# Where a block of the convolution's kernel opens within an attention step, and a ring of four PSUM banks once that kernel is done

## The chip, the cores and the metric

The kernel runs on one core of a Trainium2 chip. Its time is the device time in microseconds of one execution, and a lower time is better. TensorE is called PE below, VectorE DVE, ScalarE ACT, GpSimd POOL and SyncE SP. SP issues all of this kernel's DMA transfers. PSUM, which takes the results of matmuls, has eight banks of 128 x 512 float32, and each tile that this text names fills one bank.

## The reference, cut to what matters

Two independent operators work on sequences of length 2048 and width 448, and their outputs stand side by side.

```python
def _A_ref(u, log_A_real, A_imag, C_real, C_imag, log_dt, D_skip):
    dt = jnp.exp(log_dt)
    A = -jnp.exp(log_A_real) + 1j * A_imag
    C = (C_real + 1j * C_imag) * dt[:, None]
    P = jnp.exp((A * dt[:, None])[:, :, None] * pos[None, None, :])   # D x N x L
    K = 2.0 * jnp.einsum("dn,dnl->dl", C, P).real
    ...
    y = jnp.fft.irfft(Uf * Kf[None, :, :], L2)[:, :, :L]              # y = u convolved with K
    return y + u * D_skip[None, None, :]

def _B_ref(x, wqkv, wo):                                              # 16 heads of 28
    scores = jnp.einsum("bhqd,bhkd->bhqk", q, k) * scale
    o = jnp.einsum("bhqk,bhkd->bhqd", _softmax(scores), v)
    return o.reshape(B, S, D) @ wo
```

A makes a convolution kernel K from powers of complex numbers, and applies it in the frequency domain. B is multi-head attention.

## The kernel before

A first stage projects queries, keys and values, makes seeds for K, and leaves them in DRAM. Then comes one long loop, in which both operators are interleaved by hand: all engines keep the order in which the program issues their instructions.

**The loop.** It has 256 steps. A step handles one of 16 units (four heads times 512 queries) and one of 16 tiles of 128 keys. Within a step the tuple `ORDER` says what is issued:

```python
ORDER = ('m0', 's0', 'm1', 's1', 'v', 'f', 'pv', 'f', 'v', 'm2', 's2', 'm3', 's3', 'v')
```

- `s0` to `s3` (`s_mm`): one score matmul each into a `pss` bank, and ACT's exp of it into `p`.
- `m0` to `m3` (`max_mm`): four matmuls for the row maxima of a unit 19 steps ahead. `m0` (weights or keys named `kdif`) is read by ACT's Relu into `rl`; `m1` by DVE's combined add-and-max, which also reads `rl`; `m2` and `m3` by DVE's reductions into `mx`. This goes on while the step is below 237.
- `pv`: the product of the previous step's `p` with the values, into `po`.
- `f`: a free slot, which takes one task if one is due. In the order of the queue: urgent ends of a unit (row maxima `max_end`, with DVE's `mh`; `fin`, with sums, scaling and projections), matmuls of the convolution's kernel (`m_due`), stages of the transform of u (`u_due`, matmuls named `ua`), and the spectrum and final jobs of the convolution (`f_slot`).
- `v`: one group of DVE operations of the convolution's kernel, if one is queued.

**Blocks of the convolution's kernel.** There are 56 blocks, one every three or four steps (3.5 on average). `k_begin` opens a block at the head of a step, if the one before is through with its powers. Opening means `k_start`: three ACT copies, to `g`, to `zg` (a PSUM bank of its own, the pool `ps_g`) and to `e`. It queues nine groups for DVE (`g_powers`, one at each `v`; the lowest one needs the copies to `g` and `zg`) and nine products for POOL (`e_power`, three at the head of each of three steps, from the copy to `e`). Five steps later its matmuls (`e,g`, then `w,ko`) are due in free slots. `k_next`, at the end of a step, loads the next-but-one block's data (`sdb`) once the powers are issued.

**The ring of banks.** `w_tile` gives the next bank, in turn, to every `max_mm` and to every task in a slot. It has three banks, `pm0` to `pm2`, from the pool `ps_m`, which lives from the first stage to the end. PE waits where the bank's reader is not done. The eight banks of the loop are: three of `ps_m`, three of `ps_s` (`pss`), one of `ps_o` (`po`), one of `ps_g` (`zg`).

**Spectrum jobs.** Sixteen jobs run from about step 196 to 240, each of four tasks in slots. `forth(0)` and `last` each have 16 matmuls (`yk,mw`) into a ring bank, which DVE reads with two products `pr`. `last` then joins them: two operations `p` on DVE and two on POOL. After a gap, `back(0)` and `back(1)` (matmuls `p,mw`) are evacuated by ACT. Eight final jobs (`finish`, matmuls `zi,wb`, DVE's `ot`) follow as their spectrum is done. The block pool `g_p` is closed at the head of the first step at which nothing of the blocks is left, which is step 200.

The head and the end of a step's body before, as far as the change moves them:

```python
        k_begin(s)                       # L981, ahead of everything in the step
        ...
        for _ in range(3):               # L1003, three POOL products
            if powers["e"]:
                powers["e"].popleft()()
        ...
        k_next()                         # after the step's last operation
```

Of the kernel before, what the change touches and what calls it, by code (L numbers as in the profile page):

```python
# [7 lines left out]
F32 = mybir.dt.float32  # L8
# [5 lines left out]
PSUM = bass.MemoryType.PSUM  # L14
# [9 lines left out]
CQ = 512  # L24
# [5 lines left out]
NU = G * NQ  # L30
NS = NU * NK
LEAD = 3
ORDER = ('m0', 's0', 'm1', 's1', 'v', 'f', 'pv', 'f', 'v', 'm2', 's2', 'm3', 's3', 'v')
PB = 8
F1 = 2
FX, PD, GAP = 1, 2, 2
# [52 lines left out]
def body(ctx, tc, a, out):  # L89
# [5 lines left out]
    def pool(stack, name, bufs=1, space=None, side=None):  # L95
        kw = {} if space is None else {"space": space}
        if side:
            kw["side"] = side
        return stack.enter_context(tc.tile_pool(name=name, bufs=bufs, reuse_waits="tile", **kw))
# [18 lines left out]
    w1 = const.tile([128, 2, 128], F32, name="w1")  # L118

    att, k0_st = ExitStack(), ExitStack()  # L120
    ps_m = pool(att, "ps_m", 1, PSUM)
    n_ring = [0]

    def w_tile():

        n_ring[0] += 1
        return ps_m.tile([128, CQ], F32, name=f"pm{n_ring[0] % 3}")

    q_p = pool(att, "q_p", side="right")
    v_p = pool(att, "v_p", side="right")  # L130
# [18 lines left out]
    def load_v(g, c):  # L149
        v_g[g, c] = t = v_p.tile([128, NK // NQ, HG, 32], F32, name="v", bufs=5)  # L150
        nc.sync.dma_start(t.rearrange("p t h e -> p t (h e)"), v_d[c][:, g])
# [3 lines left out]
    def load_kd(g, j):  # L155
        kd_g[g, j] = t = kd_p[0].tile([128, CQ], F32R, name=f"kdif{j}")
        for r in range(4):
            nc.sync.dma_start(t[32 * r:32 * r + 32].bitcast(F32), kd_d[g][r % 2, 32 * j:32 * j + 32, :])
# [47 lines left out]
    with ExitStack() as st:  # L206
# [3 lines left out]
        x_p = pool(xst, "x_p")  # L210
        y_p = pool(wst, "y_p", side="right")
        w_p = pool(wst, "w_p", side="right")
        ps_t = pool(st, "ps_t", 2, PSUM)
        ps_n = pool(st, "ps_n", 2, PSUM)
        ps_x = pool(st, "ps_x", 1, PSUM)
# [327 lines left out]
    kq_st = ExitStack()  # L543
# [2 lines left out]
    g_p = pool(g_st, "g_p")  # L546
    ps_s = pool(att, "ps_s", 3, PSUM)
    ps_o = pool(att, "ps_o", 1, PSUM)
    ps_g = pool(att, "ps_g", 1, PSUM)
    k_pools = [k0_p, kq_p]  # L550

    late = [False]
# [50 lines left out]
    def load_sd(b):  # L603
        sds[b] = g_p.tile([128, SDF], F32, name="sdb", bufs=3)
        nc.sync.dma_start(sds[b], sd_d[b // BO][b % BO])

    def k_start(b):
        sd = sds[b]
        e = g_p.tile([128, 2, 16, N2], F32, name="e", bufs=2)
        g = g_p.tile([128, 2, 16, N1], F32, name="g", bufs=2)  # L610
        zg = ps_g.tile([128, CQ], F32, name="zg")
        egs[b] = e, g
        zgs[b] = zg
        nc.scalar.activation(g[:, :, :, :4], sd[:, F_G:F_Z].rearrange("p (c h e) -> p c h e", c=2, e=4), AF.Copy)
        nc.scalar.activation(zg[:, :Z_G], sd[:, SDF - Z_G:], AF.Copy)
        nc.scalar.activation(e[:, :, :, :8], sd[:, :F_G].rearrange("p (c h e) -> p c h e", c=2, e=8), AF.Copy)

    def e_power(b, i, q):

        t, m = egs[b][0], 8 << i  # L620
        zz = sds[b][:, F_Z:].rearrange("p (k f h) -> p k f h", k=6, f=3)
        if q == 0:
            zr = zz[:, i, 0, :][:, None, :, None].to_broadcast([128, 2, 16, m])
            nc.gpsimd.tensor_tensor(t[:, :, :, m:2 * m], t[:, :, :, :m], zr, ALU.mult)
        elif q == 1:
            uts[0] = g_p.tile([128, 2, 16, 32], F32, name="eu")[:, :, :, :m]
            zi = zz[:, i, 1:3, :][:, :, :, None].to_broadcast([128, 2, 16, m])
            nc.gpsimd.tensor_tensor(uts[0], t[:, ::-1, :, :m], zi, ALU.mult)
        else:
            nc.gpsimd.tensor_tensor(t[:, :, :, m:2 * m], t[:, :, :, m:2 * m], uts[0], ALU.add)  # L630

    def g_powers(b):

        t, zg = egs[b][1], zgs[b]
        zz = zg[:, :Z_G].rearrange("p (k f h) -> p k f h", k=3, f=3)
        tt = nc.vector.tensor_tensor

        def first(i, m):
            tt(t[:, :, :, m:2 * m], t[:, :, :, :m], zz[:, i, 0, :][:, None, :, None].to_broadcast([128, 2, 16, m]), ALU.mult)

        def second(i, m, c):
            n = c.stop - c.start
            u = zg[:, CQ // 2:CQ // 2 + n * 16 * m].rearrange("p (c h m) -> p c h m", c=n, m=m)
            zi = zz[:, i, 1 + c.start:1 + c.stop, :][:, :, :, None].to_broadcast([128, n, 16, m])
            tt(u, t[:, ::-1, :, :m][:, c], zi, ALU.mult)
            return lambda: tt(t[:, c, :, m:2 * m], t[:, c, :, m:2 * m], u, ALU.add)
        both, u = slice(0, 2), {}

        def lowest():
            first(0, 4)  # L650
            second(0, 4, both)()
        ops = [lowest, lambda: first(1, 8), lambda: u.update(a=second(1, 8, both)), lambda: u["a"](), lambda: first(2, 16)]
        for c in (slice(0, 1), slice(1, 2)):
            ops += [lambda c=c: u.update(a=second(2, 16, c)), lambda: u["a"]()]
        return ops
# [58 lines left out]
    def load_og(u):  # L714
        og_u[u] = og = kq_p.tile([128, G - 1, CQ], F32, name="og")
        nc.sync.dma_start(og, on_d[u % NQ][:G - 1].rearrange("g p q -> p g q"))
# [138 lines left out]
    powers = {"g": collections.deque(), "e": collections.deque()}  # L855
# [30 lines left out]
    f0_st, f1_st = ExitStack(), ExitStack()  # L886
# [62 lines left out]
    def k_begin(s_):  # L949
        if not (k_due and K0 + k_due[0] * KP <= s_ and done["mm"] >= k_due[0] - 2 and not powers["e"] and not powers["g"]):  # L950
            return
        b = k_due.popleft()
        k_start(b)
        powers["g"] += g_powers(b)
        powers["e"] += [lambda i=i, q=q: e_power(b, i, q) for i in range(3) for q in range(3)]
        p0, p1, p2 = k_mm(b)

        def m1():
            p1()
            done["mm"] = b  # L960
        m_due.extend((s_ + KD, t_) for t_ in (p0, m1, p2))
        last[0] = b
# [3 lines left out]
    def k_next():  # L966

        if last[0] is not None and not powers["e"] and not powers["g"]:
            if last[0] + 2 < NB:
                load_sd(last[0] + 2)  # L970
            last[0] = None

    def vec():
        if powers["g"]:
            powers["g"].popleft()()

    prev = None
    for s in range(NS):
        u, kt = divmod(s, NK)
        sm = s + NK + LEAD  # L980
        k_begin(s)  # L981
        if s == 12 * NK:
            k0_st.close()
            f_p["s", 0] = f_p["s", 1] = pool(f0_st, "f0_p", side="right")
            f_ready["s", 0], f_ready["s", 1] = s, NS
        if s >= 12 * NK and f_ready["s", 1] == NS and not (k_due or m_due or powers["g"] or powers["e"]):
            g_st.close()
            f_ready["s", 1] = s + F1
        if kt == 12 and u // NQ == G - 1:
            load_og(u)  # L990
        late[0] = s + NK + LEAD > NS
        if u % NQ == NQ - 1 and u < NU - 1 and kt % 4 == 2:
            load_v(u // NQ + 1, kt // 4)
        if sm < NS and sm // NK % NQ == NQ - 1 and sm % NK % 4 == 0 and sm % NK and sm // (NQ * NK) + 1 < G:
            load_kd(sm // (NQ * NK) + 1, sm % NK // 4 - 1)
        if sm < NS and sm % (NQ * NK) == 0 and sm:
            load_kd(sm // (NQ * NK), HG - 1)
        if kt % 4 == 1 and u % NQ == 1 and u // NQ + 1 < G:
            load_k(u // NQ + 1, kt // 4, k_pools[(u // NQ + 1) % 2])
        if kt == 2:  # L1000
            if u + 2 < NU:
                load_q(u + 2)
        for _ in range(3):  # L1003
            if powers["e"]:
                powers["e"].popleft()()
        ps = []
        for op in ORDER:
            if op[0] == "s":
                ps.append(s_mm(u, kt, int(op[1])))
            elif op[0] == "f":  # L1010
                slot(s)
            elif op[0] == "v":
                vec()
            elif op == "pv":
                if prev:
                    pv_step(*prev)
                    if prev[1] == NK - 1:
                        fin(prev[0], s)
            elif sm < NS:
                max_mm(sm // NK, sm % NK, int(op[1]))  # L1020
        for _ in range(FX if late[0] else 0):
            slot(s)
        if sm < NS and sm % NK == NK - 1:
            def end(un=sm // NK):
                max_end(un, w_tile())
                max_put(un)
            max_join(sm // NK)
            soon_slot(UG[0], end)
        k_next()
        prev = (u, kt, ps)  # L1030
    pv_step(*prev)
    fin(prev[0], NS)
    s = NS
# [1 line left out]
        slot(s)  # L1035
        s += 0.5
    assert not k_due and not powers["g"] and not powers["e"]
    for st in (f1_st, kq_st, f0_st, att):
        st.close()


# [55 lines left out]
```

## Time and profile before

| | us |
|---|---|
| median of three runs | 1427.25 (1426.0 to 1428.26) |
| profiled execution | 1427.0 |
| its span in the trace | 1425.2 |
| mean granted clock of PE | 0.961 of full |

In the trace, an instruction's row gives its start and length in us, the engine, and output and input tiles by name; in brackets stands how long the engine had idled and which instruction's end released it. A row "x4" merges neighbours of one kind. In a table of waits a row reads: who waited for whom, total us, times, longest. Matmul ends are modelled, so a busy PE is not a PE at its peak. Since helpers record every operation, all have line 73, and tiles tell them apart.

### The profile page before, as it was taken

The numbers are of one execution on the slowest core, as the hardware profiler recorded it, in microseconds if no ns is written. First come the engines' busy times: TensorE is split into PE (matmuls) and PEld (weight loads), VectorE is DVE, ScalarE is ACT, GpSimd is POOL, SyncE is SP. The second block draws the span as 40 slices with busy tenths as digits, with TensorE's granted clock in tenths as the row PEclk, the third lists the DMA queues.
The fourth block names the chain that finished last, engine by engine and source line by source line (L and its number), as shares of the span: only waits on it lengthen the run. The fifth ranks groups of instructions, "written<-read, shape, count | busy, mean of one in ns | idle before, by whom it ended". The sixth has DMA issues, their size and how long they took to land.

```text
span 1425.2 us, 33209 instructions
## 1 busy us (share of the span) xinstructions
PE 1273.5 (89%) x12625; PEld 707.7 (50%) x12625; DVE 978.6 (69%) x2138; ACT 974.4 (68%) x2069; POOL 830.8 (58%) x705
## 2 busy tenths in 40 slices
PE   6978856899999999999999999999988898898998
PEld 4756633445555555555555555555544444433433
DVE  5688766877778777777777878877786646645411
ACT  5867642688788888888787877878775545544553
POOL 3657650587778787778878878887861101102211
PEclk9998887899999999999999999999999999998999
DMA  6666679447663654586441316333244334435476
GB/s 190 236 235 216 225 267 249 112 98 180 150 149 85 152 151 122 157 200 165 140 91 40 92 36 150 89 79 84 55 136 134 112 106 144 154 110 164 134 199 175
DMA packets 200729, 205.37 MB, mean 144 GB/s; under 512 B 96632, under 2 KB 159160, under 8 KB 198520
## 3 DMA queue, kind: packets, MB, share of 16 engines
q1 hardware_dynamic: 200568, 203.23, 51.4%
q8 instruction: 100, 1.64, 0.5%
q14 instruction: 61, 0.50, 0.1%
HBM read 120.73 MB, written 82.18 MB: 142 GB/s over the span
## 4 chain that ended last, share of the span: by engine, by line
PE 58%; DVE 23%; ACT 7%; POOL 6%; issue 3%; DMA 3%; SPq 0%; ACTq 0%; DVEq 0%; POOLq 0%
PE pm L73 34%; PE po L73 13%; PE pss L73 11%; DVE mx L73 5%; DVE g L73 4%; DVE rl L73 3%; DVE p L73 3%; POOL qhat L73 3%; ACT p L73 2%; DVE pr L73 2%; ACT rl L73 2%; DVE tri L73 1%; DVE px L73 1%; DVE zg L73 1%; POOL x_e L73 1%
## 5 line engine op out<-in xcount | busy, mean ns | idle before, releaser
L73 ACT ACTIVATE p<-pss 128x512 f32<-128x512 f32 x1024 | 563.0, 607 | 162.4 <-PE pss L73 153.4
L73 DVE TENSOR_REDUCE mx<-pm 128x1 f32<-128x512 f32 x500 | 321.3, 683 | 141.5 <-PE pm L73 140.6
L73 PE MATMUL pss<-qhat,khat 128*128 128x512 f32 x1024 | 405.2, 402 | 3.2 <-ACT p L73 3.2
L73 PE MATMUL pm<-khat,qhat 128*128 128x512 f32 x749 | 335.3, 451 | 62.0 <-DVE mx L73 60.2
L73 POOL TENSOR_TENSOR e<-e,sdb 128x256 f32<-128x256 f32 x168 | 201.6, 1200 | 185.2 <-ACT e L73 129.6
L73 PE MATMUL po<-p,v 128*32 128x512 f32 x2048 | 278.8, 612 | 0.0
L73 PEld LDWEIGHTS pm<-khat,qhat 128*128 128x128 f32 x749 | 142.4, 190 | 247.3 <-DVE mx L73 114.9
L73 POOL TENSOR_TENSOR e<-e,eu 128x256 f32<-128x256 f32 x168 | 248.3, 1478 | 13.2
L73 DVE CUSTOM_DVE_ANT_0 rl<-pm,rl 128x512 f32<-128x512 f32 x249 | 171.5, 689 | 107.2 <-ACT rl L73 86.9
L73 PEld LDWEIGHTS pss<-qhat,khat 128*128 128x128 f32 x1024 | 192.0, 190 | 46.1 <-ACT p L73 12.8
L73 POOL TENSOR_TENSOR eu<-e,sdb 128x256 f32<-128x256 f32 x168 | 201.9, 1202 | 0.0
L73 POOL TENSOR_TENSOR p<-pr,pr 64x448 f32<-64x448 f32 x32 | 40.6, 1269 | 237.5 <-DVE pr L73 236.3
L73 ACT ACTIVATE rl<-pm 128x512 f32<-128x512 f32 x249 | 150.2, 603 | 32.3 <-PE pm L73 31.6
L73 DVE TENSOR_TENSOR g<-g,zg 128x128 f32<-128x128 f32 x392 | 162.7, 415 | 5.0
L73 PE MATMUL pm<-kdif,qhat 128*128 128x512 f32 x249 | 103.7, 417 | 14.9 <-DVE ot L73 4.0
L73 PEld LDWEIGHTS pm<-e,g 128*32 128x32 f32 x3584 | 64.0, 110 | 52.2 <-issue 34.2
L73 DVE TENSOR_TENSOR zg<-g,zg 128x128 f32<-128x128 f32 x224 | 87.3, 390 | 3.5
L73 ACT ACTIVATE y<-pm 128x448 f32<-128x448 f32 x48 | 26.3, 549 | 80.4 <-PE pm L73 54.1
L73 PEld LDWEIGHTS po<-p,v 128*32 128x32 f32 x2048 | 57.5, 111 | 43.8 <-issue 39.1
L73 PE MATMUL pm<-e,g 128*32 128x64 f32 x3584 | 72.8, 220 | 0.0
L73 PEld LDWEIGHTS pm<-kdif,qhat 128*128 128x128 f32 x249 | 47.3, 190 | 43.5 <-PE pss L73 9.7
L73 PE MATMUL pm<-xh,wh 112*128 112x512 f32 x128 | 54.5, 430 | 13.5 <-DVE tl L73 6.3
(137 smaller groups left out, 1545.8 us busy)
## 6 DMA issues: line engine op xcount, KB each, us to landing
sdb<-sd SPq DMA_DIRECT2D x56, 336.0 KB
qhat<-q SPq DMA_DIRECT2D x64, 256.0 KB
khat<-k SPq DMA_DIRECT2D x64, 256.0 KB
sd<-sg SPq DMA_DIRECT2D x8, 1456.0 KB
mw<-in_mw SPq DMA_DIRECT2D x16, 512.0 KB
sd<-qhat SPq DMA_DIRECT2D x8, 896.0 KB
yk<-yk SPq DMA_DIRECT2D x56, 128.0 KB
yu_d<-ub SPq DMA_DIRECT2D x64, 112.0 KB
```

The source lines that it names most:

```text
L73: i = f(*args, **kw)
```

## The change

The opening of a block moves into `ORDER` as an operation `k`, right behind `pv`. There `k_next`, `k_begin` and the three POOL products of the step are issued, so that they come between the step's two free slots. The ring's pool is no longer one for the whole kernel: the first stage has its own (`ps_w`), and the loop has `ps_m`, opened together with `ps_g`. At step 200, where `g_p` is closed, `ps_g` and `ps_m` are closed too, and a pool `ps_f` of four banks takes their place; from there `w_tile` gives one of its four in turn.

```diff
-ORDER = ('m0', 's0', 'm1', 's1', 'v', 'f', 'pv', 'f', 'v', 'm2', 's2', 'm3', 's3', 'v')
+ORDER = ('m0', 's0', 'm1', 's1', 'v', 'f', 'pv', 'k', 'f', 'v', 'm2', 's2', 'm3', 's3', 'v')
...
-    ps_m = pool(att, "ps_m", 1, PSUM)
-    n_ring = [0]
+    ps_w, n_ring = [None, 3], [0]
 
     def w_tile():
 
         n_ring[0] += 1
-        return ps_m.tile([128, CQ], F32, name=f"pm{n_ring[0] % 3}")
+        return ps_w[0].tile([128, CQ], F32, name=f"pm{n_ring[0] % ps_w[1]}")
...
         w_p = pool(wst, "w_p", side="right")
+        ps_w[0] = pool(st, "ps_w", 1, PSUM)
         ps_t = pool(st, "ps_t", 2, PSUM)
...
     ps_o = pool(att, "ps_o", 1, PSUM)
-    ps_g = pool(att, "ps_g", 1, PSUM)
+    ps_st = ExitStack()
+    ps_g = pool(ps_st, "ps_g", 1, PSUM)
+    ps_w[0] = pool(ps_st, "ps_m", 1, PSUM)
...
-        k_begin(s)
         if s == 12 * NK:
...
         if s >= 12 * NK and f_ready["s", 1] == NS and not (k_due or m_due or powers["g"] or powers["e"]):
             g_st.close()
+            ps_st.close()
+            ps_w[:] = pool(ps_st, "ps_f", 4, PSUM), 1
             f_ready["s", 1] = s + F1
...
-        for _ in range(3):
-            if powers["e"]:
-                powers["e"].popleft()()
         ps = []
         for op in ORDER:
...
             elif op[0] == "v":
                 vec()
+            elif op == "k":
+                k_next()
+                k_begin(s)
+                for _ in range(3):
+                    if powers["e"]:
+                        powers["e"].popleft()()
             elif op == "pv":
...
-    for st in (f1_st, kq_st, f0_st, att):
+    for st in (ps_st, f1_st, kq_st, f0_st, att):
         st.close()
```

`k_next()` at the end of the step in the kernel before stays where it is; behind a `k` that has already loaded, it finds nothing to do.

## The prediction

> **What bounds the kernel now.** I read the page's engine shares first, then busy time by stage, then the table of waits for the stages that the change touches, then the order of time inside single steps.
>
> ```profile
> span 1425.2 us, 33209 instructions
> ...
> PE 1273.5 (89%) x12625; PEld 707.7 (50%) x12625; DVE 978.6 (69%) x2138; ACT 974.4 (68%) x2069; POOL 830.8 (58%) x705
> ```
>
> TensorE (PE) is busy for 89% of the span, but that is a mean over unlike stages. The rows below are stretches of the attention loop: from us, to us, length, then busy time of PE, PEld, DVE, ACT and POOL, and the granted clock. The first two lie where blocks of the convolution's kernel are made (steps 0 to about 199), the third where the spectrum work runs (about 200 to 236).
>
> ```profile
> 480.00:690.00 210.00, 204.76 (x2380) 109.94 (x2373) 156.56 (x372) 174.76 (x409) 162.38 (x129) 1.00 0.59 159
> ...
> 870.00:1059.00 189.00, 176.08 (x2082) 98.18 (x2082) 150.03 (x357) 148.47 (x327) 157.81 (x123) 1.00 0.37 90
> ```
> ```profile
> 1079.00:1318.00 239.00, 205.12 (x1800) 99.01 (x1799) 136.79 (x237) 116.53 (x221) 33.25 (x26) 0.91 0.42 136
> ```
>
> Up to 690 us PE fills 204.8 of 210 us: both free slots of a step hold matmuls, and a late other engine rarely shows. From 690 to 1059 us the slots are half empty, and PE idles for 12.9 of 189 us while DVE, ACT and POOL each sit near 80%: here their order within the step decides. From 1079 us PE idles for 34 of 239 us, and its granted clock falls to 0.91. What ends PE's idle time there:
>
> ```profile
> PE pm L73 <- DVE mx L73: 24.0, 10, 2.5
> ...
> PE pm L73 <- DVE ot L73: 4.0, 1, 4.0
> PE pm L73 <- DVE pr L73: 3.2, 13, 0.3
> ...
> PE pm L73 <- DVE mh L73: 2.4, 1, 2.4
> ```
>
> Those 33.6 us are all PE waiting for DVE to release a `pm` bank. From 690 to 1059 us the same wait is shorter and more frequent, and DVE in turn waits for ACT's `rl`:
>
> ```profile
> DVE rl L73 <- ACT rl L73: 28.5, 46, 1.3
> ...
> PE pm L73 <- DVE mx L73: 24.4, 30, 1.2
> ```
>
> **Part 1: a block opens in the middle of a step.** PE's instruction order is unchanged, and so are the 56 opening steps (0, 4, 7, 11, ...: four and three steps apart in turn). What moves: `k_start`'s three ACT copies go from ahead of `rl` to behind the step's second exp and first free slot; the nine POOL products follow; the nine DVE groups start one `v` later, so the last one falls on the first `v` of the fourth step. `load_sd` is issued on SP about half a step later, behind that step's loads and first slot, for a block that opens at least three steps on; `sdb` has three buffers, so nobody waits for it. POOL's own order is kept and it starts later by under 2 us. Its products are used five steps after the opening, while they take under three, so that slack of about two steps (8 us) hides it; without it PE would pay the 2 us per block.
>
> One opening step four steps after the last, before the change:
>
> ```profile
> 881.57 0.31 ACT L73 ACTIVATE g<-sdb 128x128 f32<-128x128 f32 x1
> 881.77 0.30 ACT L73 ACTIVATE zg<-sdb 128x144 f32<-128x144 f32 x1
> ...
> 882.29 0.60 ACT L73 ACTIVATE rl<-pm 128x512 f32<-128x512 f32 x1
> ...
> 882.76 2.07 ACT L73 ACTIVATE p<-pss 128x512 f32<-128x512 f32 x4
> ...
> 882.91 0.69 DVE L73 CUSTOM_DVE_ANT_0 rl<-pm,rl 128x512 f32<-128x512 f32 x1 [1.32 <-PE po L73]
> ...
> 883.53 0.28 DVE L73 TENSOR_TENSOR g<-g,zg 128x128 f32<-128x128 f32 x1
> ...
> 884.18 0.74 DVE L73 TENSOR_TENSOR g<-g,zg 128x128 f32<-128x128 f32 x2
> ...
> 884.84 1.28 DVE L73 TENSOR_REDUCE mx<-pm 128x1 f32<-128x512 f32 x2
> ...
> 885.58 0.50 PE L73 MATMUL pm<-khat,qhat 128*128 128x512 f32 x1 [1.11 <-DVE mx L73]
> ```
>
> The copies hold ACT for 0.72 us (881.57 to 882.29), so DVE idles 1.32 us ahead of `rl`; the first powers and then `mx` come late, and PE stands 1.11 us for the bank that the first `mx` frees. Now with the change. `rl` takes the copies' place at 881.57; exps follow 0.47 us later (882.29 to 882.76) and 0.52 us apart (2.07/4): 882.04, 882.56; with an empty slot the copies start at 883.07, and `zg` (0.20 later, 0.30 long) ends at 883.57. DVE is through with `rl` by then, waits, and begins the lowest power at about 883.62 instead of 883.53. But in between it now has one group less: from 883.53 to the second power's start (884.18 + 0.28 + 0.04 = 884.50) are 0.97 us, after which `mx` starts: 884.59 less the small overlap, against 884.84. Gain about 0.27 us.
>
> Three steps after the last opening, `zg`'s copy had also to wait for the previous block's last addition on DVE:
>
> ```profile
> 893.38 0.41 DVE L73 TENSOR_TENSOR g<-g,zg 128x256 f32<-128x256 f32 x1
> 893.43 0.31 ACT L73 ACTIVATE g<-sdb 128x128 f32<-128x128 f32 x1
> ...
> 893.82 0.29 ACT L73 ACTIVATE zg<-sdb 128x144 f32<-128x144 f32 x1
> ...
> 896.89 1.28 DVE L73 TENSOR_REDUCE mx<-pm 128x1 f32<-128x512 f32 x2
> ```
>
> With the change: `rl` at 893.43, DVE's `rl` from 894.05, 0.61 later that addition (0.41, to 895.07); copies from 893.43 + 0.47 + 2 x 0.52 = 894.94, `zg` done by 895.43; lowest power 895.48, `mx` 896.45 against 896.89. Gain 0.44 us. From 690 us there are 26 openings, 13 of each kind: 13 x 0.27 + 13 x 0.44 = 9.2 us.
>
> Before 690 us the first slot mostly holds work that ACT evacuates, and that now stands ahead of the copies:
>
> ```profile
> 307.99 0.58 ACT L73 ACTIVATE ub<-pm 128x448 f32<-128x448 f32 x1
> ...
> 309.11 1.28 DVE L73 TENSOR_REDUCE mx<-pm 128x1 f32<-128x512 f32 x2
> ...
> 309.85 0.50 PE L73 MATMUL pm<-khat,qhat 128*128 128x512 f32 x1 [0.37 <-DVE mx L73]
> ```
>
> The evacuation pushes the copies back by its 0.5 us pace; the same count puts `mx` at 309.32, 0.21 us late, after a four-step gap, and level after a three-step gap. Of these 30 openings some have an empty slot and gain; I take 1 us lost, between 6 us lost (30 x 0.21) and 6 us gained.
>
> **Part 2: four PSUM banks for `w_tile`.** From step 200 (powers, products and their matmuls all done) `zg`'s bank joins the ring. The other pool moves only re-lay banks at the loop's start, on tiles long read: nothing, at most 1 us either way. In a ring of three, tile n waits for the reader of n-3; in a ring of four for n-4's, which the ring of three had already demanded one tile sooner. So no single wait gets longer. A stall at full clock, three steps ahead of the switch, serves as the measure:
>
> ```profile
> 1064.02 2.66 DVE L73 TENSOR_TENSOR p<-pr,pr 64x448 f32<-64x448 f32 x2
> ...
> 1066.61 1.27 DVE L73 TENSOR_REDUCE mx<-pm 128x1 f32<-128x512 f32 x2
> 1067.34 0.50 PE L73 MATMUL pm<-khat,qhat 128*128 128x512 f32 x1 [2.50 <-DVE mx L73]
> ...
> 1068.88 0.94 PE L73 MATMUL pm<-p,mw 128*32 128x224 f32 x16
> ```
>
> DVE joins the spectrum (2.66 us) ahead of `mx`, and PE's second `khat` matmul of the next step waits. With a fourth bank that matmul, its score matmul and, where the next slot is empty, `po` run during the joins; then the slot's `p,mw` needs that same `mx`. PE resumes at 1067.34 with `p,mw` instead of reaching it at 1068.88: 1.5 us gained, and the idle stretch shrinks from 2.5 to about 1.5 us. Of the ten `mx` stalls, four are of this kind (first slot of the next step empty). In the other six that slot needs the bank ahead of `po`: gain 0.7 us each (the `khat` and score matmuls with their weight loads), leaving 1.7 us idle where it was 2.15 (three) and 2.0 where it was 2.5 (three). The `mh` and `ot` stalls give 0.5 us each by the same move, and half of the `pr` waits 1.6 us. Sum: 4 x 1.5 + 6 x 0.7 + 2 x 0.5 + 1.6 = 12.8 us.
>
> The larger half may be the clock. These rows are consecutive stretches of 3.4 us, PE's busy time first, clock third from the end:
>
> ```profile
> 1082.90:1086.30 3.40, 1.46 (x6) 0.58 (x4) 3.35 (x4) 2.17 (x4) 2.53 (x2) 1.00 0.52 198
> 1086.30:1089.70 3.40, 2.58 (x10) 0.91 (x14) 2.06 (x5) 0.60 (x1) 0.00 (x0) 0.51 0.00 0
> 1103.40:1106.80 3.40, 1.75 (x22) 1.11 (x26) 2.89 (x5) 1.37 (x4) 0.51 (x1) 1.00 0.22 81
> 1106.80:1110.20 3.40, 3.40 (x32) 2.05 (x24) 1.39 (x3) 2.18 (x5) 0.00 (x0) 1.00 0.29 97
> ```
>
> A stretch with 1.46 us of work is followed by one at half clock; one with 1.75 us is not. So the line lies between 1.65 and 1.94 us of idle time in a stretch. At 0.91 over 239 us, 0.09 x 239 = 21.5 us of full speed are lost, 12 to 13 half-speed stretches of 1.7 us each. After the change, the 1.5 us stalls should never cross the line, the 1.7 us ones in a quarter of the cases, the three of 2.0 us and `mh` in about half (it depends on how the stall lies to the stretches), `ot`'s 3.5 us still does: 0.8 + 2 + 1 = about 4 stretches, 7 us. Gain 14 us, between 0 and 20.
>
> [...]
>
> **The sum.** The profiled execution took 1427.0 us (span 1425.2 and 1.8 around it), 0.25 below the median: 1427.0 - 9.2 + 1 - 12.8 - 14 = 1392 us.
>
> **Rivals.**
> 1. The clock stays as low: stalls of 1.5 to 2 us still tip it, or it has another cause. For it: the line is read off few stretches. Against: the 1103.40 row. Time 1392 + 14 = 1406.
> 2. The fourth bank buys nothing, because DVE itself is late: the joins only push the next step's `rl` and `mx`. For it: DVE is the last engine in all those waits. Against: DVE has 137 us of work in 239. Time 1427 - 8 = 1419. [...]
> 3. Slower: the opening copies become DVE's wait. The lowest power stands in DVE's queue ahead of both `mx`; if the copies come later than counted (behind the exps and a second evacuation of 0.58 us, 0.21 + 0.58 = 0.8 us per block), PE waits at the same bank in all 56 blocks: 45 us lost against 27 gained by the pool, 1445. It decides from 27/56 = 0.5 us per block on. For it: 0.2 us is already counted where the slot is full. Against: from 690 us the slot is empty, and until then PE is 97% full by itself.
> 4. Nothing moves by more than 0.2% (about what a measurement of this kernel can tell from no change): the losses of part 1 eat what rival 2 leaves.
>
> **Numbers.** Forecast 0.64, around 1392, by itself 1379 to 1403 (a clock gain of 7 to 20 us gives 1386 to 1399; part 1 adds 6 either way, less where both ends meet). Rival 1: 0.17. Rival 2: 0.08. Rival 3: 0.08. Rival 4: 0.03. The range 1377 to 1412 takes in the forecast and rival 1, and leaves out 2, 3 and 4: about 0.19. Faster: 0.64 + 0.17 + 0.08 = 0.89; same 0.03; slower 0.08.
>
> **What would show it.** Part 1: DVE's wait for ACT's `rl` falls well below 28.5 us between 690 us and the end of the blocks, a wait of DVE's powers for ACT's `zg` of 0.3 to 0.8 us per block appears, and PE's `mx` wait falls from 24.4 to about 15 us. Part 2: PE's long waits for `mx` now stand at `p,mw` or another slot's first matmul, near 1.5 to 2 us, and the granted clock of that stage is about 0.97. I am wrong if those stalls keep their 2.5 us, if the clock stays at 0.91, or if `zg` waits exceed 1 us.

## The result and the profile after

The changed kernel takes 1366.6 us (median of six runs, 1363.7 to 1367.7), against 1426.4 us before (six runs, 1424.3 to 1428.3). The ratio is 0.958, with a 95% interval of 0.957 to 0.959. The direction was forecast, the size was not: 60 us came where 34 were expected, and the time lies below the range.

The profile's head for the changed kernel shows the same work in a shorter span:

```profile
span 1364.9 us, 33230 instructions
...
PE 1243.5 (91%) x12625; PEld 707.2 (52%) x12625; DVE 980.3 (72%) x2138; ACT 968.6 (71%) x2069; POOL 831.0 (61%) x705
```

Here are the stretches that answer to those of before (columns as there: from, to and length in us, busy time of PE, PEld, DVE, ACT and POOL, granted clock).

```profile
480.00:690.00 210.00, 205.35 (x2419) 112.21 (x2422) 159.49 (x378) 176.71 (x414) 165.60 (x132) 1.00 0.60 162
870.00:1043.00 173.00, 162.84 (x1960) 93.38 (x1959) 142.11 (x338) 140.42 (x311) 148.07 (x117) 1.00 0.38 91
1064.00:1259.00 195.00, 182.58 (x1803) 95.99 (x1803) 136.31 (x237) 113.80 (x222) 34.27 (x27) 0.99 0.52 167
```

The last row is the spectrum stage: 195 us where the row of before had 239. PE's idle time in it fell from 239 - 205.1 = 33.9 to 195 - 182.6 = 12.4 us, so 21.5 us came from waits. Its busy time, for the same 1,800 matmuls, fell by 22.5 us, most of it because the granted clock rose from 0.91 to 0.99: before, 43.1 us of the busy time ran at half clock, after it 3.4. In the trace before, a row of sixteen `p,mw` took 1.72 us at half clock (1120.54) and 0.94 at full (1068.88). Counted as half of the difference, which is an estimate, the clock's part is 19.8 us. What is left of the waits in that stage (who waited for whom, total us, times, longest):

```profile
PE pm L73 <- DVE mx L73: 5.0, 6, 1.0
PE pm L73 <- DVE ot L73: 3.5, 1, 3.5
PE pm L73 <- ACT rl L73: 1.7, 4, 0.8
```

The waits for `mx` fell from 24.0 to 5.0 us, and the longest from 2.5 to 1.0. A wait for ACT's `rl` is new. Now the waits of the stretch from 687 to 1043 us, in which the blocks open next to half-empty slots:

```profile
PE pm L73 <- DVE mx L73: 20.1, 29, 1.3
...
DVE g L73 <- ACT zg L73: 15.7, 24, 1.2
DVE rl L73 <- ACT rl L73: 14.5, 38, 0.9
```

DVE's wait for `rl` has halved (28.5 before), and its wait for `zg` has appeared. Measured between the starts of steps in the traces, the stage shares out as follows: steps 0 to 103 took 425.2 us (428.7 before), steps 103 to 192 339.0 (352.1), and steps 200 to 237 194.8 (239.7). In the traces before and after, every stretch of one granted clock but the last of each lasts 3.41 us or a multiple of it. Counted in stretches of 3.41 us, the 2.5-us stall at step 197 lay across an edge before (1064.84 to 1067.34, edge at 1065.86), with 1.27 us of PE's idle time in the stretch ahead of the edge and 1.48 in the one behind it, and the clock stayed at 1.00. After the change it lies inside one stretch (1048.33 to 1050.84 in 1047.56 to 1050.97), which has 2.57 us of idle time, and a stretch at 0.50 follows. By half of its length, an estimate, that gives back 1.7 us between steps 192 and 200.

### The profile page after: what moved, and what is told of

Its sections match the earlier page's. It is cut to its first block, busy times and chain, and to the rows that moved or that the text cites. A ratio compares the mean times of both kernels' runs of the same rounds, so it can differ in the third digit from the quotient of the medians.

```text
span 1364.9 us, 33230 instructions
## 1 busy us (share of the span) xinstructions
PE 1243.5 (91%) x12625; PEld 707.2 (52%) x12625; DVE 980.3 (72%) x2138; ACT 968.6 (71%) x2069; POOL 831.0 (61%) x705
## 3 DMA queue, kind: packets, MB, share of 16 engines
q8 instruction: 100, 1.64, 0.5%
## 4 chain that ended last, share of the span: by engine, by line
PE 58%; DVE 16%; ACT 11%; POOL 5%; DMA 5%; issue 3%; SPq 0%; ACTq 0%; DVEq 0%; POOLq 0%
PE pm L73 34%; PE po L73 13%; PE pss L73 12%; ACT p L73 6%; DVE mx L73 3%; POOL qhat L73 3%; DVE g L73 2%; ACT rl L73 2%; DVE p L73 2%; DMA khat<-k 2%; DVE tri L73 1%; DVE pr L73 1%; DVE px L73 1%; POOL x_e L73 1%; DVE sg L73 1%
## 5 line engine op out<-in xcount | busy, mean ns | idle before, releaser
L73 PE MATMUL pm<-khat,qhat 128*128 128x512 f32 x749 | 329.7, 443 | 41.5 <-DVE mx L73 36.1
L73 PE MATMUL po<-p,v 128*32 128x512 f32 x2048 | 271.8, 598 | 0.0
L73 PE MATMUL pm<-kdif,qhat 128*128 128x512 f32 x249 | 100.9, 405 | 2.4 <-DMA v<-v 1.3
L73 DVE TENSOR_TENSOR pr<-pm,ub 128x448 f32<-128x448 f32 x64 | 37.0, 619 | 32.7 <-PE pm L73 32.7
```

The source lines that it names most:

```text
L73: i = f(*args, **kw)
```

## The experiments

Two questions were open. Why did the pool alone give some 16 us more than the 26.8 forecast for it? And what in the opening's move makes its gain, the copies that left the head of ACT, or the DVE group that fell behind the `mx` reductions? All runs of an experiment stand against the kernel before (medians of 1426.1 us in both groups of runs).

### The two halves alone: `k_only` and `pool_only`

`k_only` is the changed kernel without the pool of four:

```diff
             g_st.close()
-            ps_st.close()
-            ps_w[:] = pool(ps_st, "ps_f", 4, PSUM), 1
```

> The changed opening of the blocks alone; the ring of three named banks stays to the end. Theory A (the two parts add up, and the difference of the traces is divided at step 200): 1366.6 + 45 = 1412 us (1408 to 1416), with step 200 reached near 1064 us as in the changed kernel, ten mx stalls of 2 to 2.5 us and ten to thirteen half-clock stretches behind it. Theory B (opening only pays because the later stage follows): 1420 to 1427.

`pool_only` has the pools of the changed kernel, and the opening at the head of the step as before.

> The pool of four alone; blocks open at the head of the step as before. Theory A (the parts add up): 1426.4 - 45 = 1381 us (1378 to 1385), the same step times as the changed kernel from step 200 on within 0.1 us each. Theory B (the pool's gain needs the other phase of the loop, for instance for the clock's stretches): 1390 or more.

Measured: `k_only` 1411.6 us (ratio 0.990, 0.988 to 0.991), `pool_only` 1382.9 us (0.970, 0.967 to 0.972). The halves bring 14.6 and 43.2 us, together 57.8 of the 59.8, so they add up to within 2 us. The spectrum stage of `k_only`, then that of `pool_only`:

```profile
1064.50:1302.00 237.50, 203.66 (x1803) 99.48 (x1801) 137.62 (x236) 116.69 (x222) 34.09 (x27) 0.91 0.42 138
```
```profile
1079.00:1272.00 193.00, 180.78 (x1802) 95.11 (x1800) 135.97 (x236) 113.72 (x221) 34.59 (x27) 1.00 0.52 169
```

Without the pool the stage and its clock are those of before. With it alone, they are those of the changed kernel, but for one stretch at half clock (1.00 against 0.99).

### In turn or by choice: `ring4` and `free3`

The new pool's four banks share one tile name (`pm0`, since every count leaves remainder 0 by 1), whereas the pool before had three names that come strictly in turn. So the new four do not come in turn, as the section on the change has it. `ring4` gives the fourth bank and keeps the turn:

```diff
-            ps_w[:] = pool(ps_st, "ps_f", 4, PSUM), 1
+            ps_w[:] = pool(ps_st, "ps_f", 1, PSUM), 4
```

> The changed kernel, but from step 200 on the four banks are four named tiles taken strictly in turn, where the changed kernel's pool of four tiles of one name gives out whichever bank the build counts as free first. Theory A (what the prediction lacked is that the bank is chosen, not taken in turn): the slot task behind the spectrum's join waits for DVE's mx again, about 1.5 us in four places and 1.7 to 2.0 us in six, PE's waits for mx in that stage come to 15 to 20 us instead of 5.0, three to six half-clock stretches of 3.4 us come back, and the time is 1367 + 13 + 5 = 1385 us (1378 to 1392). Theory B (the fourth bank alone does it, and the prediction only sized the stalls too large): within 3 us of 1367.

`free3` gives the one name and keeps three banks:

```diff
-            ps_w[:] = pool(ps_st, "ps_f", 4, PSUM), 1
+            ps_w[:] = pool(ps_st, "ps_f", 3, PSUM), 1
```

> The changed kernel, but the pool from step 200 on has three tiles of one name, so zg's bank is not used: the choice of the bank without the fourth bank. Theory A (the choice is worth as much as the bank): the second khat matmul behind a join takes the bank that ACT's rl frees instead of the one of mx, waits about 1 us instead of 2.5, few half-clock stretches remain, and the time is 1380 to 1392. Theory B (the fourth bank is what counts): 1405 to 1412, as with the ring of three.

Measured: `ring4` 1384.1 us (0.970, 0.969 to 0.972), `free3` 1389.7 us (0.975, 0.973 to 0.977). The spectrum stage of `ring4`, then its waits there, then the same two of `free3`:

```profile
1064.00:1274.00 210.00, 184.59 (x1802) 96.72 (x1801) 136.49 (x237) 113.65 (x221) 34.00 (x26) 0.98 0.48 155
```
```profile
PE pm L73 <- DVE mx L73: 19.7, 11, 2.5
PE pm L73 <- DVE ot L73: 3.5, 1, 3.5
PE pm L73 <- DVE mh L73: 2.2, 1, 2.2
```
```profile
1065.00:1281.00 216.00, 192.47 (x1800) 95.17 (x1799) 136.73 (x236) 116.22 (x220) 33.89 (x26) 0.97 0.46 151
```
```profile
PE pm L73 <- DVE mx L73: 7.9, 10, 1.3
PE pm L73 <- ACT rl L73: 5.7, 11, 0.8
```

A strict ring of four takes 27.5 us off the stage's 237.5 us in `k_only`, and its `mx` waits still sum to 19.7 us. The name alone, with no fourth bank, cuts those waits from 24.0 to 7.9 us, and puts 5.7 us of waits for `rl` in their place. Both together leave 5.0 and 1.7. What the name does can be read at a single step, 204. First `ring4`:

```profile
1082.45 2.69 DVE L73 TENSOR_TENSOR p<-pr,pr 64x448 f32<-64x448 f32 x2
...
1083.78 0.61 ACT L73 ACTIVATE rl<-pm 128x512 f32<-128x512 f32 x1
...
1085.06 1.28 DVE L73 TENSOR_REDUCE mx<-pm 128x1 f32<-128x512 f32 x2
1085.88 0.96 PE L73 MATMUL pm<-p,mw 128*32 128x224 f32 x16 [1.78 <-DVE mx L73]
```

The same step of the changed kernel:

```profile
1081.24 2.69 DVE L73 TENSOR_TENSOR p<-pr,pr 64x448 f32<-64x448 f32 x2
...
1082.58 0.60 ACT L73 ACTIVATE rl<-pm 128x512 f32<-128x512 f32 x1
...
1083.28 0.96 PE L73 MATMUL pm<-p,mw 128*32 128x224 f32 x16 [0.38 <-issue]
1083.86 0.68 DVE L73 TENSOR_REDUCE mx<-pm 128x1 f32<-128x512 f32 x1
```

DVE joins the spectrum for 2.69 us in both, ahead of `mx`. In the strict ring the slot's `p,mw` is due on the bank that this `mx` must free, and waits 1.78 us. With one name, the built program puts `p,mw` on the bank that `m0` of the same step used and that ACT's `rl` has just left (1082.58 + 0.60 = 1083.18). It starts at 1083.28, before `mx` has begun. The bank sequence of the built programs says the same: for this step's `m0`, `m1` and `p,mw` the strict ring gives banks 6, 7 and 4 (which the previous step's `m2` holds), the pool of one name 6, 7 and 6 again. A pool of one name is thus no ring. Its order of banks fits a build that gives out the bank that it counts as free first; that rule is read off the order, not shown.

### The choice from the first step of the loop: `free_all`

```diff
-    ps_w[0] = pool(ps_st, "ps_m", 1, PSUM)
+    ps_w[:] = pool(ps_st, "ps_m", 3, PSUM), 1
```

> The changed kernel with its loop pool ps_m also under one name with three banks, so that the choice of bank that the last stage has holds from the first step of the loop; nothing else is changed. If the choice helps wherever DVE holds a bank, the 20.1 us of waits for mx between 690 us and step 192 halve: 1350 to 1360 us. If it helps only where free slots are filled behind a long DVE job (as in the last stage), steps with an empty slot still bring the next matmul to the bank that mx holds: 1362 to 1368 us.

Measured: 1373.7 us (0.963, 0.962 to 0.965), 7 us slower than the changed kernel, which neither theory expected. Its waits from 692 to 1053 us:

```profile
PE pm L73 <- DVE mx L73: 19.2, 27, 1.3
...
PE pm L73 <- ACT rl L73: 5.8, 12, 0.9
```

The waits for `mx` stay (20.1 in the changed kernel), and 5.8 us of waits for `rl` come on top. By steps, it lost 5.0 us between 103 and 192, where PE's idle time grew by 4.9. Up to 103 it lost 5.8: 3.2 are idle time, and some 2.6, by the same estimate of half, come from 5.3 us at half clock at the loop's start (1.4 us before, none in the changed kernel; why they differ was not shown). Between 192 and 200 it gained 3.0, by that estimate 1.7 of them because it has no half-clock stretch there, where the changed kernel has one of 3.41 us. In step 107, for one, the slot's `e,g` takes the bank of its own step's `m0`, which `rl` has yet to leave (bank 7 for both in the built program):

```profile
709.17 0.65 PE L73 MATMUL pm<-e,g 128*32 128x64 f32 x32 [0.42 <-ACT rl L73]
```

Here, with no long DVE job that holds the other banks, the turn was the better order.

### Where the block opens: `k_before_v`, `k_after_v`, `k_late`

All three are the changed kernel with `k` at another place:

```diff
-ORDER = ('m0', 's0', 'm1', 's1', 'v', 'f', 'pv', 'k', 'f', 'v', 'm2', ...)
+ORDER = ('m0', 's0', 'm1', 's1', 'k', 'v', 'f', 'pv', 'f', 'v', 'm2', ...)   # k_before_v
+ORDER = ('m0', 's0', 'm1', 's1', 'v', 'k', 'f', 'pv', 'f', 'v', 'm2', ...)   # k_after_v
+ORDER = ('m0', 's0', 'm1', 's1', 'v', 'f', 'pv', 'f', 'v', 'k', 'm2', ...)   # k_late
```

> The changed kernel with the opening k one operation earlier than the first v, right behind the second score matmul, instead of behind pv. The copies still stand behind the second exp on ACT, but DVE gets its first group of a block at the first v, as before the change, so three groups stand ahead of the later mx reductions again. Theory A (the gain of opening mid-step comes from the DVE group that moved behind the mx reductions): the 14.6 us that the opening brought are gone, 1377 to 1385 us, and PE's wait for mx between 690 us and step 192 is back near 24 us. Theory B (it comes from the copies leaving the head of ACT, ahead of rl): the time stays at 1365 to 1370 us and that wait near 20 us.

> The changed kernel with the opening k directly behind the first v, ahead of the first free slot and pv. DVE's order is that of the changed kernel; only the copies on ACT stand ahead of the first slot's evacuation instead of behind it. Theory A (DVE's order makes the gain): from step 103 on the same, 14 to 17 us gained to step 192; before that the evacuation no longer pushes the copies back, so up to 30 x 0.2 = 6 us more: 1361 to 1368 us. Theory B (ACT's order makes it): evacuations in the 30 blocks of the first half come 0.7 us later and PE waits for their bank: 1367 to 1380 us.

> The changed kernel with the opening k behind the second free slot and the second v. DVE's lowest power then comes behind both mx reductions of the opening step, and one group returns to the second v of the fourth step. Theory A (what stands in DVE's queue ahead of mx makes the time): DVE's waits for zg (15.7 us from 690 us to step 192, 27.0 us before) no longer delay mx; between 0 and 0.3 us more gained per block: 1352 to 1367 us. Theory B (only the head of ACT mattered): the same time, 1365 to 1369 us, whatever the zg waits do.

| | us, median | ratio, 95% interval | steps 0 to 103 | steps 103 to 192 |
|---|---|---|---|---|
| before | 1426.1 | | 428.7 | 352.1 |
| `k_before_v` | 1382.8 | 0.970 (0.969 to 0.971) | 429.0 | 349.9 |
| changed kernel | 1366.6 | 0.958 (0.957 to 0.959) | 425.2 | 339.0 |
| `k_after_v` | 1355.7 | 0.951 (0.949 to 0.952) | 418.3 | 335.6 |
| `k_late` | 1344.4 | 0.943 (0.941 to 0.944) | 419.0 | 323.3 |

`k_before_v` and `pool_only` differ in ACT's order, but in both DVE gets a block's first group ahead of the same `mx`, and both take 1382.8 to 1382.9 us. So taking the copies off ACT's head is worth nothing by itself that the total shows. It does shorten DVE's waits for `rl` (18.7 us from 690 to 1057 us, 28.5 before), but PE's waits for `mx` there stay (24.2 us, 24.4 before), and so does PE's idle time between steps 103 and 192 (26.9 us, 26.2 before). The 2.2 us by which that stage is shorter lie in PE's busy time. Here is the opening at 881 us in `k_before_v`, the same block as the prediction's, and the step behind it:

```profile
882.01 0.29 DVE L73 TENSOR_TENSOR g<-g,zg 128x128 f32<-128x128 f32 x1 [0.66 <-ACT zg L73]
...
882.34 0.29 DVE L73 TENSOR_TENSOR zg<-g,zg 128x128 f32<-128x128 f32 x1
...
882.66 0.74 DVE L73 TENSOR_TENSOR g<-g,zg 128x128 f32<-128x128 f32 x2
...
883.32 1.28 DVE L73 TENSOR_REDUCE mx<-pm 128x1 f32<-128x512 f32 x2
...
884.06 0.50 PE L73 MATMUL pm<-khat,qhat 128*128 128x512 f32 x1 [1.13 <-DVE mx L73]
```

The lowest power now waits for `zg`, `mx` still waits behind it and the group after it, and PE stands 1.13 us, as it did before (1.11). The changed kernel at the same block:

```profile
872.71 0.33 ACT L73 ACTIVATE zg<-sdb 128x144 f32<-128x144 f32 x1
...
873.07 0.29 DVE L73 TENSOR_TENSOR g<-g,zg 128x128 f32<-128x128 f32 x1 [0.66 <-ACT zg L73]
...
873.72 0.29 DVE L73 TENSOR_TENSOR g<-g,zg 128x128 f32<-128x128 f32 x1
873.93 1.28 DVE L73 TENSOR_REDUCE mx<-pm 128x1 f32<-128x512 f32 x2
...
874.66 0.50 PE L73 MATMUL pm<-khat,qhat 128*128 128x512 f32 x1 [0.69 <-DVE mx L73]
```

One group fewer stands between the lowest power and `mx`, and PE's wait is 0.69 us. In `k_late` none stands there:

```profile
857.39 0.33 ACT L73 ACTIVATE zg<-sdb 128x144 f32<-128x144 f32 x1
...
857.54 1.29 DVE L73 TENSOR_REDUCE mx<-pm 128x1 f32<-128x512 f32 x2 [0.45 <-PE pm L73]
...
858.50 0.39 PE L73 MATMUL pm<-khat,qhat 128*128 128x512 f32 x1
...
858.75 0.28 DVE L73 TENSOR_TENSOR g<-g,zg 128x128 f32<-128x128 f32 x1
```

DVE reduces as soon as PE has the scores, the powers follow, and PE's `m1` of the next step (858.50) doesn't wait. Over `k_late`'s stretch from 680 us to step 192, PE is busy for 321.0 of 323 us, and its waits for `mx` from 680 to 1020 us are down to 1.0 us:

```profile
680.00:1003.00 323.00, 320.97 (x3814) 183.31 (x3813) 279.74 (x668) 271.49 (x607) 293.60 (x232) 1.00 0.37 87
```
```profile
DVE rl L73 <- ACT rl L73: 19.2, 54, 0.8
PE pm L73 <- DVE mx L73: 1.0, 5, 0.2
```

So the first theory held: what stands in DVE's queue ahead of `mx`, and how long it waits there, makes the time. Its sizes were too careful twice. `k_late`, 22 us below the changed kernel, lies under the 1352 us that the theory allowed at best; 15.7 us of that came between steps 103 and 192. `k_after_v`, 11 us below, lies under the theory's 1361 us. It has DVE's order of the changed kernel, and its copies no longer wait behind a slot's evacuation, so that the power ahead of `mx` gets them sooner: its waits for `zg` up to 678 us sum to 15.1 us, against 27.0 up to 688 us in the changed kernel, PE's waits for `mx` there sum to 4.7 against 10.1 us, and 6.9 us were gained before step 103. `k_late` is the fastest version run.

## Why the prediction was wrong, step by step

**The failed step: the ring of four.** The prediction put: "In a ring of three, tile n waits for the reader of n-3; in a ring of four for n-4's". The diff gives the new pool a single name, and then no turn exists. "Then the slot's `p,mw` needs that same `mx`" followed from the turn, and fell with it. `ring4`, in which the step is true, shows that the sum was nearly right for the kernel that it described: the stage lost 27.5 us, where the forecast had 12.8 + 14 = 26.8. PE's busy time at half clock in the stage, in `k_only` and then in `ring4`, sums to:

```profile
sum 40.96, PE 39.05 PEld 16.78 DVE 12.62 ACT 11.68 POOL 0.45; mean PE 3.90 PEld 1.68 DVE 1.26 ACT 1.17 POOL 0.05
```
```profile
sum 10.24, PE 9.48 PEld 3.95 DVE 4.37 ACT 1.33 POOL 0.00; mean PE 3.16 PEld 1.32 DVE 1.46 ACT 0.44 POOL 0.00
```

Half of the difference, 14.8 us, is by the same estimate the clock's part (forecast 14). That leaves 12.7 us for the waits (forecast 12.8): 33.8 - 25.4 = 8.4 us of idle time, and 4.3 us of PE's busy time at full clock, which could not be placed. The single stalls fit less well, so the near hit of the sum is partly luck. Four fell from 2.51 to 1.63 us (1.5 forecast; the prediction counts 1.5 us gained on each, though by its own account their idle time shrinks by 1.0). Another three fell from 2.15 to 1.78 (1.7 forecast; step 204 is one of them). Three more, at steps 209, 229 and 234, kept 2.53 us, where 2.0 was forecast; the `pr` waits, of which half was to go, went altogether. One stall of the first kind, at step 201, and one of the last, at step 209:

```profile
1072.70 0.96 PE L73 MATMUL pm<-p,mw 128*32 128x224 f32 x16 [1.63 <-DVE mx L73]
...
1111.65 0.43 PE L73 MATMUL pm<-sel,o 128*32 128x4 f32 x32 [2.53 <-DVE mx L73]
```

So the forecast's error on the pool is what it left out: the choice of bank brought 15 us more (210 to 195), 13 of them idle time, and most of the rest the clock (one stretch at half clock instead of three). That `w_tile` takes its banks in turn was not doubted, though the diff's last argument (`4, PSUM), 1`) and the order of the built program's banks showed otherwise.

**The clock.** It came to 0.99 instead of 0.97, since one half-clock stretch was left in the stage, not four: the one behind `ot`'s stall of 3.5 us, as put. `ring4` has three and 0.98. The forecast had the clock halve from somewhere between 1.65 and 1.94 us of idle time in such a stretch. That was nearly right, but the traces show no single line. In `ring4` and `free3`, each stretch with the one that follows it:

```profile
1083.00:1086.41 3.41, 1.63 (x17) 1.05 (x19) 3.37 (x5) 2.37 (x5) 1.58 (x2) 1.00 0.72 272
1086.41:1089.82 3.41, 3.41 (x42) 2.15 (x33) 1.55 (x4) 1.68 (x4) 0.00 (x0) 1.00 0.21 70
1182.00:1185.41 3.41, 1.42 (x18) 0.95 (x22) 3.38 (x6) 1.63 (x4) 0.94 (x1) 1.00 0.92 312
1185.41:1188.82 3.41, 3.41 (x31) 1.35 (x20) 0.33 (x2) 0.54 (x1) 0.00 (x0) 0.50 0.24 79
```
```profile
1110.00:1113.41 3.41, 1.62 (x41) 0.74 (x44) 3.37 (x5) 1.65 (x3) 1.48 (x2) 1.00 0.02 6
1113.41:1116.82 3.41, 3.41 (x26) 1.76 (x19) 0.80 (x4) 1.17 (x2) 0.00 (x0) 0.50 0.02 5
```

1.78 us of idle time kept the clock in one (1083.00) and 1.79 halved it in another (1110.00); in `free3`, 1.59 us did so as well (1263.60). The clock gave the 19.8 us above, and before the change all half-clock stretches of the stage but those behind `ot`'s stall of 4.0 us follow stalls of 2.1 to 2.5 us.

**Part 1, the place right and the size too small.** The gain is where the prediction put it: at `m1` of the step after the opening, which it calls the second `khat` matmul. It was 1.11 - 0.69 = 0.42 us there for the block shown, not 0.27: `mx` begins 873.93 - 873.07 = 0.86 us after the lowest power, not 0.97. From step 103 to 192 the sum is 13.1 us, not 9.2. PE's listed idle time gives 7.1 of them (352.1 - 325.9 before, 339.0 - 319.9 after). The other 6 lie in PE's busy time at full clock: the rows of many matmuls are a little shorter (a mean of 446 ns for `khat` before, 440 after). Why could not be placed. Before 690 us the forecast was 1 us lost; the traces show 3.5 gained, of which 0.7 is half of 1.4 us at half clock at the loop's start (262.3 to 263.7) that the changed kernel's trace doesn't have, and 0.5 idle time; the cause of the rest stays open. The evacuation did push the copies back (an average wait of 1.0 us for `zg` there), but the 0.21 us per full slot that this was to cost PE did not appear: its waits for `mx` there are 10.1 us, against 9.6 before, and the counterpart of the wait of 0.37 us that the prediction shows at 309.85 us is 0.36 us long.

```profile
310.55 0.50 PE L73 MATMUL pm<-khat,qhat 128*128 128x512 f32 x1 [0.36 <-DVE mx L73]
```

**What fitted.** DVE's wait for `rl` fell well below 28.5 us (14.5), the `zg` wait appeared (0.65 us each on average from 687 us; the 1.0 us before that is above the forecast), and PE's `mx` wait fell, though to 20.1 and not to about 15. "I am wrong if `zg` waits exceed 1 us" was too strong a sign: single ones reached 1.2 and 2.0 us, and the kernel gained nevertheless.

**The rivals.** Rival 1 fell with the clock of 0.99. Rivals 2 and 4 fell with `pool_only`'s 43 us. Rival 3 had the right mechanism and the wrong price: the lowest power does stand ahead of both `mx` and does wait for the copies. But one group fewer behind it pays for that, and what the power and its wait cost ahead of `mx` is seen only against `k_late`: 22 us, hidden in a kernel that still became faster.

## What to carry to other kernels

Before counting which bank a tile waits for, look at how the pool is named: several names used by remainder are a strict ring, and several buffers of one name need not come in turn, which can skip a bank that a late engine holds (15 us of the last stage here), but can also choose worse than the turn (7 us lost in `free_all`). When an operation is moved within a step, ask what it then stands ahead of in the queue of the engine whose buffer release PE waits for. Here it was worth nothing in the total to take the copies off ACT's head while DVE still had to wait for them ahead of `mx` (`k_before_v`), and 38 us to let `mx` go first as well (`k_late`).

## What the runs showed of the hardware

In the traces before (1059 to 1390 us) and after (1040 to 1340 us), the granted clock halved behind each of the thirteen full-clock stretches of 3.41 us in which PE idled for 1.98 us or more, and behind none in which it idled for 1.64 us or less; there were none between. `ring4` and `free3` have some: 1.78 us kept the clock, 1.79 halved it, and 1.59 halved it too. A stall of 2 us was thus followed by up to 1.7 us more of lost time, an estimate that takes half of the 3.41-us stretch behind it. Of the kernel before, 44.4 us of the spectrum stage ran at half clock, of the changed kernel 3.4 us.
